# An attention and feed-forward kernel whose softmax weights are rounded and selected one head ahead of their use, with the loads and the exchange of squares moved in the step

## The chip, the cores and the metric

The kernel runs on one core of a Trainium2 chip. The metric is the device time of one execution in microseconds (us); lower is better. The core has TensorE (PE, with its weight loads as PEld), VectorE (DVE), ScalarE (ACT), GpSimd (POOL) and SyncE (SP), which here issues nearly every DMA. Each engine works through its own instructions in order and waits on semaphores for the others.

## The reference

Sliding-window attention with 4 sink keys feeds a feed-forward block, all in float32:

```python
B, H, S, D = q.shape            # 4, 8, 768, 64; n_sink 4, window 128
scores = scale * np.matmul(q, k.transpose(0, 1, 3, 2))
keep = is_sink | in_window      # the first 4 keys, or the 128 up to the query
a = softmax(np.where(keep, scores, -1e9))
x = (a @ v).transpose(0, 2, 1, 3).reshape(B * S, H * D)   # 3072 x 512
h = x @ w_in                                               # 512 x 2048
g = np.maximum(h, 0.0) + np.log1p(np.exp(-np.abs(h)))      # softplus
out = g @ w_out                                            # 2048 x 512
```

## The kernel before

The 3072 rows are cut into 12 chunks of 256 queries, three to a batch; a chunk has 8 heads. For a head, a block of 128 queries needs its own 128 keys and those of the block before, and because the window is 128 long each row keeps exactly one key of each pair (own key k, old key k); so the softmax runs on 128 + 8 columns (8 for the sinks), and the weights are later parted by a triangular select. To keep float32 accuracy, operands of matmuls are split into a rounded high part and a residue: `th` and `tl` of the transposed weights, `vv` of the values, `qkh` and `kl` of queries and keys, `gh` and `gl` of the gate, `xh` and `xl` of the attention's output.

The work is software-pipelined by hand. After an opening (`START`, a list of parts that also loads and splits the weights), a loop runs a step i for each head, and a string names the parts of a step in order; a part's number in the table `parts` says how many heads ahead of i it works. The order of the parts is the program order on every engine. Written for step i, the parts are: `L` loads query and key of head i+6, `G` the values (every second head); `p` splits the queries and keys of head i+5 (`qkh` on ACT, then `qkh`, `kl` on DVE); `S`, `T`, `N` are scores, softmax and normalisation of head i+4; `X` (swap) lets DVE transpose the normalised weights in squares of 32 into the one buffer `xf`, and SP write them to DRAM as `rows` by four DMAs; `x` (swapped) reads them back as `u`; `W` (weights_t) rounds `u` to `th` on ACT, and on POOL makes the residue `tl` and four triangular selects into `pt`, which has two buffers; `V` multiplies `pt` by the values on PE; `O` adds up and splits the output; `k` and `K` handle the sinks of four heads (`sa`, `ts`, `sk`). The dense block works 8 steps behind: `U` (up, 24 matmuls), `F` (softplus on ACT), `P` (gate), `R` (residue), and `D`, `E` (down, 6 matmuls each); the stores of a chunk's output are issued in `E`. In the opening the number stands behind the letter: `X18` is the transpose of head 18.

`xf` is one buffer, so a transpose waits until the four DMAs of the one before have read it; `u` has one buffer for even and one for odd heads; `qk` has two buffers, `vr` one.

```python
        nc.vector.transpose(squares.rearrange("p (f j q) -> p f j q", j=CH, q=32), a)
        for e in range(P // 32):
            nc.sync.dma_start(rows[:, e].rearrange("(f k) r -> k f r", k=32), src)
        # swapped:
        nc.sync.dma_start(u[:].rearrange("p e j q -> p (e j q)"), self.u[h][:].rearrange("p e r -> p (e r)"))
```

Of the kernel before, what the change touches and what calls it, by code (L numbers as in the profile page):

```python
# [20 lines left out]
B, H, S, D = 4, 8, 768, 64  # L21
# [521 lines left out]
def _weight_check(c, s, k, half):  # L543

    if not c.w64:
        return
    w = c.w[s, k, half][:, 0].rearrange("p n w -> p (n w)")  # L550
    o = 2 * (2 * s + k) + half
    for e, op in enumerate((ALU.min, ALU.max)):
        c.nc.vector.tensor_reduce(c.room[:, e, o : o + 1], w, mybir.AxisListType.X, op, apply_absolute_value=True)
# [71 lines left out]
def _fast(c):  # L625
# [6 lines left out]
    att = [_Attention(c, k) for k in range(n)]  # L632
# [3 lines left out]
    def call(lst, name, every=1, *args):  # L636
        def run(i):
            k, e = divmod(i, H)
            if 0 <= i < n * H and e % every == 0:
                getattr(lst[k], name)(e // every, *args)  # L640

        return run
# [67 lines left out]
    def idle(k):  # L710
# [11 lines left out]
        "N": (call(att, "normalise"), G),  # L722
        "p": (call(att, "split"), G + 1),
        "q": (call(att, "split_v", 2), 1),
        "W": (call(att, "weights_t"), 0),
        "X": (call(att, "swap"), 2),
        "x": (call(att, "swapped"), 1),
        "k": (call(att, "sink_weights", G), 0),
        "K": (call(att, "sink", G), 0),
        "V": (call(att, "values"), 0),  # L730
# [16 lines left out]
    with c.tc.manual_schedule():  # L747
        for h in (0, 2):
            att[0].load(h)
        _constants(c)  # L750
        att[0].load_v(0)
        att[0].load_sinks()
        att[0].load(4)
        att[0].load_v(1)
        att[0].load(6)
        c.turn = 0
        c.upper = [c.lp.tile([P, WH], I32, tag=f"vs{e}", name=f"upper{e}", bufs=1) for e in range(2)]
        for t in c.upper:
            c.nc.gpsimd.memset(t[:], 0)
        c.word_ps = [c.ps_acc.tile([P, WH], I32, tag=f"acc{e}", name=f"word_ps{e}") for e in range(2)]  # L760
        for part in c.START.split():
            parts[part[0]][0](int(part[1:] or 0))
        for i in range(2 * H + 1, (n + 1) * H + lag + 1):
            for part in "xXJjGL" + c.STEADY[i % H == 0]:
                run, ahead = parts[part]
                run(i + ahead)
            if i >= 2 * H + lag and i % 2 == 0 and checks:
                _weight_check(c, *checks.pop(0))
            if i == n * H + lag:
                for e in checks:  # L770
                    _weight_check(c, *e)
                _fast_signs(c)
            if i == n * H + 2 * lag:
                _fast_flag(c)


def _fast_signs(c):

    nc = c.nc
    c.col = col = c.const.tile([P, 3], F32, name="flag_col")  # L780
    nc.vector.tensor_reduce(col[:, 0:1], c.stats[:, : c.nchunks * CH * H], mybir.AxisListType.X, ALU.max)
    for e, (op, lim, beyond) in enumerate(((ALU.min, 2.0**-119, ALU.is_lt), (ALU.max, 2.0**121, ALU.is_ge))):
        m = col[:, e + 1 : e + 2]
        nc.vector.tensor_reduce(m, c.room[:, e], mybir.AxisListType.X, op)
        nc.vector.tensor_scalar(m, m, lim, BIG, beyond, ALU.mult)
        nc.vector.tensor_tensor(col[:, 0:1], col[:, 0:1], m, ALU.max)


def _fast_flag(c):

    nc, cp = c.nc, c.const
    row = c.ps_t.tile([1, P], F32, tag="t", name="flag_row")
    nc.tensor.transpose(row[:], c.col[:, 0:1], c.ident[:])
    f = cp.tile([1, 2], F32, name="flag_f")
    ok, u = f[:, 0:1], f[:, 1:2]
    nc.vector.tensor_reduce(ok, row[:], mybir.AxisListType.X, ALU.max)
    nc.vector.tensor_scalar(ok, ok, 9.0e8, None, ALU.is_lt)
    for src, lim, op in ((c.ns, float(NS), ALU.is_le), (c.wd, 1.0, ALU.is_ge), (c.wd, float(P), ALU.is_le)):
        nc.vector.tensor_scalar(u, src[:1], lim, None, op)
        nc.vector.tensor_tensor(ok, ok, u, ALU.mult)  # L800
    c.flag = cp.tile([1, 1], I32, name="flag_i")
    nc.vector.tensor_copy(c.flag[:], ok)
# [126 lines left out]
def _kernel(tc, a, out):  # L929
# [7 lines left out]
    with ExitStack() as keep:  # L937
# [12 lines left out]
        with ExitStack() as st:  # L950
            pool = lambda n, bufs: st.enter_context(tc.tile_pool(name=n, bufs=bufs))
            psum = lambda n, bufs: st.enter_context(tc.tile_pool(name=n, bufs=bufs, space=bass.MemoryType.PSUM))
            c.xp, c.mp, c.stg = pool("xp", 2), pool("mp", 2), pool("stg", 4)
            c.lp, c.ap, c.sp = pool("lp", 2), pool("ap", 2), pool("sp", 2)
            c.dp = st.enter_context(tc.tile_pool(name="dp", bufs=4, space=bass.MemoryType.DRAM))
            c.ps_acc, c.ps_t, c.ps_x = psum("ps_acc", 1), psum("ps_t", 1), psum("ps_x", 1)
            fronts = {}

            def scores_pool(name, bufs, to):
                side = "right" if name[-1] == "s" else "left"  # L960
                p = tc.tile_pool(name=name, bufs=bufs, space=bass.MemoryType.PSUM, side=side, reuse_waits="tile")
                return to.enter_context(p)

            def follow(name):
                fronts[name].close()
                return scores_pool(name, 2, st)

            for n in ("ps_s", "ps_h"):
                fronts[n] = st.enter_context(ExitStack())
            c.front_s, c.front_h = (scores_pool(f"front{n[2:]}", 1, own) for n, own in fronts.items())  # L970
            c.follow, c.ps_s, c.ps_h, c.idle = follow, None, None, None
            c.xf = c.sp.tile([P, 2, CT], F32, name="xf", bufs=1)
            with tc.manual_schedule(engines=ORDERED):
                _fast(c)
# [12 lines left out]
Ctx.WH = "APPPAAPAPPPPAAVAPAPAVAAVPAAAVAPA"  # L987
Ctx.WL = "PPPVVPPVPPVVVPVPVPPVVVPPVPPVVPPV"
Ctx.STEADY = (
    "kWUqYpKSFTRDVPONE",  # L990
    "SWTkpUKERDNFPqYVO",
)
Ctx.START = """
W0 N12 V14 V4 O4 V6 V0 S0 N6 V12 w j4 V2 N14 W14 O0 V10 N0 w w L8 O2 N2 S1 J0 w w w L10 L12 w T0 T1 S2 G4 w V8
# [4 lines left out]
W11 W4 T14 G16 c l c W2 D0 a d S15 d P2 l L19 U3 a L20 T15 W13 R1 E0 c l S16 c N15 D1 O9 E1 k12 R2 E2 F3 d l d  # L999
d a a T16 D2 P3 c a U4 L22 c l l a c d N16 R3 D3 d p17 c a p18 F4 d d V11 l l a K12 c d O11 a U5 N8 l l G18  # L1000
S17 F5 c T17 P4 c W10 l R4 p19 V13 O13 W15 X16 a a d S18 l a U6 E3 d T18 D4 P5 d c S19 T19 R5 l l d c p20 F6 q16 l
l P6 J16 N18 E4 V15 x16 a O15 U7 N19 S20 W16 c c c U8 D5 E5 F7 N17 X17 k16 N10 T20 R6 F8 P7 x17 X18 R7 P8 K16 E6 d d d L21 p21
a D6 N20 V16 W6 l l O16
"""


# [44 lines left out]
```

## Time and profile before

| what | value |
|---|---|
| median of 3 runs | 718.83 us (715.72 to 719.13) |
| profiled execution, its time | 718.53 us |
| its span, first to last instruction | 716.6 us |
| busy: PE, DVE, ACT, POOL | 676.0, 531.9, 476.5, 445.9 us |
| granted TensorE clock, mean | 0.993 |

The time is the span and about 2 us around it. PE is the busiest engine, and its matmuls overlap, so that a busy PE isn't one at its peak; where PE stands still, the row of the instruction that ends the wait says for how long and on whom. The opening takes the first 104 us of the span, the loop up to 660 us, and from there on only the dense block of the last chunk is left.

### The profile page before, as it was taken

Reading aid. Unit: us, or ns where it says so; the run is one execution under the profiler, and the core shown is the slowest. Engines: PE = TensorE matmul, PEld = TensorE weight load, DVE = VectorE, ACT = ScalarE, POOL = GpSimd, SP = SyncE. Lnnn points to the kernel's source line nnn. Section 1 sums busy time; section 2 is a strip of 40 time slices with the busy share of each in tenths; the row PEclk is TensorE's granted clock in tenths of the full one; section 3 lists DMA queues with packets and bytes.
Section 4 is the critical chain, followed back from the end, with each engine's and each line's share of the span. In section 5 each row is a group of like instructions: output and inputs, shape, how many; then the busy total and the mean of one; then the engine's idle time right before and its main releaser. Section 6 shows DMA issues by size and latency. Waiting matters only on the chain.

```text
span 716.6 us, 14271 instructions
## 1 busy us (share of the span) xinstructions
PE 676.0 (94%) x4319; PEld 596.2 (83%) x4319; DVE 531.9 (74%) x1461; ACT 476.5 (66%) x1213; POOL 445.9 (62%) x817
## 2 busy tenths in 40 slices
PE   6999968999999999899999989999999999999996
PEld 3588857888988889789989979888988988899995
DVE  6999947878878788778788778877788777753331
ACT  6999746767768667667777666767676676754431
POOL 7775556777666675676766676686766766674110
PEclk9999989999999999999999999999999999999999
DMA  8996124334344443433443443534433433420001
GB/s 315 362 403 177 52 61 114 99 90 126 101 105 116 116 104 91 135 94 91 130 113 93 132 111 88 146 84 111 116 97 101 134 94 96 115 67 8 30 1 34
DMA packets 97656, 83.33 MB, mean 116 GB/s; under 512 B 51876, under 2 KB 79140, under 8 KB 97572
## 3 DMA queue, kind: packets, MB, share of 16 engines
q1 hardware_dynamic: 97428, 82.35, 39.9%
q8 instruction: 36, 0.59, 0.4%
q14 instruction: 48, 0.39, 0.2%
q10 hardware_dynamic: 144, 0.00, 0.0%
HBM read 65.53 MB, written 16.78 MB: 115 GB/s over the span
## 4 chain that ended last, share of the span: by engine, by line
PE 34%; DVE 15%; ACT 14%; POOL 10%; DMA 7%; issue 6%; SPq 4%; DVEq 0%; ACTq 0%; POOLq 0%
PE h L574 16%; DMA qk<-qk 6%; PE acc L611 5%; PE acc L612 5%; PE acc L613 5%; PE x L444 3%; SPq L378 3%; ACT a L293 2%; POOL tl L67 2%; POOL pt L406 2%; POOL a L318 2%; POOL pt L409 2%; ACT mt L582 2%; DVE xt L464 2%; ACT mt L583 2%
## 5 line engine op out<-in xcount | busy, mean ns | idle before, releaser
L574 PE MATMUL h<-xh,wi 128*128 128x256 f32 x1536 | 246.7, 283 | 0.3 <-DVE mt L589 0.3
L574 PEld LDWEIGHTS h<-xh,wi 128*128 128x128 f32 x1536 | 215.7, 191 | 7.1 <-issue 0.9
L574 PE MATMUL h<-xl,wi 128*128 128x256 f32 x768 | 154.7, 283 | 0.0
L611 PE MATMUL acc<-wo,gh 128*128 128x512 f32 x384 | 153.2, 399 | 0.0
L613 PE MATMUL acc<-wo,gl 128*128 128x512 f32 x384 | 151.2, 394 | 0.7 <-DVE gl L67 0.7
L612 PE MATMUL acc<-wo,gh 128*128 128x512 f32 x384 | 151.6, 395 | 0.0
L63 POOL TENSOR_SCALAR gh<-mt 128x512 fp32r<-128x512 f32 x88 | 54.5, 619 | 140.3 <-DVE mt L589 125.1
L574 PEld LDWEIGHTS h<-xl,wi 128*128 128x128 f32 x768 | 119.6, 192 | 0.0
L581 ACT ACTIVATE mt<-h 128x512 f32<-128x512 f32 x96 | 57.4, 598 | 84.7 <-PE h L574 74.3
L318 POOL TENSOR_SCALAR a<-a,rc 128x128 f32<-128x128 f32 x156 | 60.4, 399 | 57.5 <-DVE rc L307 46.8
L589 DVE SCALAR_TENSOR_TENSOR mt<-h,mt 128x512 f32<-128x512 f32 x96 | 65.6, 684 | 41.0 <-ACT mt L583 28.1
L613 PEld LDWEIGHTS acc<-wo,gl 128*128 128x128 f32 x384 | 72.5, 189 | 18.6 <-DVE gl L67 1.9
L293 ACT ACTIVATE a<-a,stats 128x136 f32<-128x136 f32 x192 | 76.0, 397 | 16.0 <-DVE stats L292 15.6
L611 PEld LDWEIGHTS acc<-wo,gh 128*128 128x128 f32 x384 | 72.7, 189 | 12.7
L67 DVE TENSOR_TENSOR qkh<-qk,qkh 64x256 fp32r<-64x256 f32 x80 | 46.7, 584 | 46.9 <-ACT qkh L59 45.8
L612 PEld LDWEIGHTS acc<-wo,gh 128*128 128x128 f32 x384 | 72.9, 190 | 9.5
L59 ACT CAST qkh<-qk 128x656 fp32r<-128x656 f32 x80 | 59.0, 738 | 31.4 <-DMA qk<-qk 31.0
L67 DVE TENSOR_TENSOR gl<-mt,gh 128x512 fp32r<-128x512 f32 x96 | 73.6, 767 | 4.3 <-POOL gh L63 4.0
L67 POOL TENSOR_TENSOR tl<-u,th 128x256 f32<-128x256 f32 x80 | 63.7, 796 | 7.7 <-ACT th L59 7.7
L444 PE MATMUL x<-pt,vv 128*128 128x256 f32 (+1 forms) x216 | 50.4, 336 | 17.1 <-POOL pt L409 16.6
L582 ACT ACTIVATE mt<-mt 128x512 f32<-128x512 f32 x96 | 60.7, 633 | 3.1
L583 ACT ACTIVATE mt<-mt 128x512 f32<-128x512 f32 x96 | 60.7, 632 | 3.1
(193 smaller groups left out, 1203.4 us busy)
## 6 DMA issues: line engine op xcount, KB each, us to landing
qk<-qk SPq DMA_DIRECT2D x160, 164.0 KB, 3.1
rows<-xf SPq DMA_DIRECT2D x320, 32.0 KB, 1.6
u<-rows SPq DMA_DIRECT2D x80, 128.0 KB, 2.6
vr<-v SPq DMA_DIRECT2D x32, 192.0 KB, 2.7
out<-o SPq DMA_DIRECT2D x24, 256.0 KB, 2.3
qk<-qk SPq DMA_DIRECT2D x8, 328.0 KB, 6.4
vr<-v SPq DMA_DIRECT2D x16, 128.0 KB, 2.3
wi00r<-w SPq DMA_DIRECT2D x1, 511.8 KB
```

The lines of the kernel that those rows point to most:

```text
L59: nc.scalar.copy(out, in_)
L67: (nc.vector if eng == "V" else nc.gpsimd).tensor_tensor(out, a, b, ALU.subtract)
L293: nc.scalar.activation(a, a, AF.Exp, bias=nm, scale=-1.0, accum_out=total)
L318: (nc.vector if eng == "V" else nc.gpsimd).tensor_scalar(a, a, rc[:, j : j + 1], 0.0, ALU.mult, ALU.add)
L444: nc.tensor.matmul(x[:, :, o], w, pt[:, :, m], start=False, stop=n == 2, skip_group_check=True)
L574: nc.tensor.matmul(h[:, j], wt, x, start=k == 0, stop=k >= len(prods) - 2, skip_group_check=True)
L582: nc.scalar.activation(t[:], t[:], AF.Exp, scale=-1.0)
L583: nc.scalar.activation(t[:], t[:], AF.Ln, bias=1.0)
L589: nc.vector.scalar_tensor_tensor(t[:], h[:], 0.0, t[:], ALU.max, ALU.add)
L611: nc.tensor.matmul(acc[:], gh[:, j, q], wh, start=f == 0, stop=False, skip_group_check=True)
L612: nc.tensor.matmul(acc[:], gh[:, j, q], wl, start=False, stop=False, skip_group_check=True)
L613: nc.tensor.matmul(acc[:], gl[:, j, q], wh, start=False, stop=f == 2 * FP - 1, skip_group_check=True)
```

## The change

`W` works one head further ahead (i+1 where it was i), and so do `x` (i+2) and `X` (i+3). `x` and `X` no longer stand first in a step: `x` comes behind the loads `G` and `L`, and `X` stands in the middle of the step, behind `F`. The last lines of the opening are rewritten to fit: the load `L21` stands ahead of `x16`, `x17` and `X18` ahead of `T20`, and `W17`, `x18` and `X19` are now in the opening.

```diff
-        "W": (call(att, "weights_t"), 0),
-        "X": (call(att, "swap"), 2),
-        "x": (call(att, "swapped"), 1),
+        "W": (call(att, "weights_t"), 1),
+        "X": (call(att, "swap"), 3),
+        "x": (call(att, "swapped"), 2),
...
-            for part in "xXJjGL" + c.STEADY[i % H == 0]:
+            for part in "JjGLx" + c.STEADY[i % H == 0]:
...
-    "kWUqYpKSFTRDVPONE",
-    "SWTkpUKERDNFPqYVO",
+    "kWUqYpKSFTXRDVPONE",
+    "SWTkpUKERDNFXPqYVO",
...
-l P6 J16 N18 E4 V15 x16 a O15 U7 N19 S20 W16 c c c U8 D5 E5 F7 N17 X17 k16 N10 T20 R6 F8 P7 x17 X18 R7 P8 K16 E6 d d d L21 p21
-a D6 N20 V16 W6 l l O16
+l P6 J16 N18 E4 V15 L21 x16 a O15 U7 N19 S20 W16 c c c U8 D5 E5 F7 N17 X17 k16 N10 x17 X18 T20 R6 F8 P7 x18 X19 R7 P8 K16 E6 d d d p21
+a D6 N20 W17 V16 W6 l l O16
```

What this does to the engines' own orders is seen at two places. The first is a step of the loop. On POOL, in step 18 (heads of chunk 2: the number behind the tile's name is the chunk, the next one the head, or for `gh` the slice of the dense block), before:

```order
L318 TENSOR_SCALAR a2_1_1349<-a2_1_1349,rc2_1_1350 128x128 x2
L67 TENSOR_TENSOR tl2_2_1553<-u2_2_1427,th2_2_1551 128x256
L406 AFFINE_SELECT pt2_2_1555<-th2_2_1551 128x2x128
L409 AFFINE_SELECT pt2_2_1555<-th2_2_1551 128x2x128
L406 AFFINE_SELECT pt2_2_1555<-tl2_2_1553 128x2x128
L409 AFFINE_SELECT pt2_2_1555<-tl2_2_1553 128x2x128
L63 TENSOR_SCALAR gh1_2_1625<-mt1_2_1598 128x512
```

and now:

```order
L318 TENSOR_SCALAR a2_1_1360<-a2_1_1360,rc2_1_1361 128x128 x2
L67 TENSOR_TENSOR tl2_3_1564<-u2_3_1450,th2_3_1562 128x256
L406 AFFINE_SELECT pt2_3_1566<-th2_3_1562 128x2x128
L409 AFFINE_SELECT pt2_3_1566<-th2_3_1562 128x2x128
L406 AFFINE_SELECT pt2_3_1566<-tl2_3_1564 128x2x128
L409 AFFINE_SELECT pt2_3_1566<-tl2_3_1564 128x2x128
L63 TENSOR_SCALAR gh1_2_1642<-mt1_2_1609 128x512
```

The work of POOL between the normalisation and the gate is the same, but for head 3 instead of head 2. On DVE, in step 19, before:

```order
L553 TENSOR_REDUCE room_64<-wi00_343 128x1 x2
L374 STREAM_TRANSPOSE xf_105<-a2_1_1349 128x256
L67 TENSOR_TENSOR qkh3_0_1691<-qk3_0_1548,qkh3_0_1691 64x256
L67 TENSOR_TENSOR kl3_0_1694<-qk3_0_1548,qkh3_0_1691 128x400
L285 COPY_PREDICATED s2_7_0_1696<-diag_133,s2_7_0_1696 128x128
L285 COPY_PREDICATED s2_7_1_1699<-diag_133,s2_7_1_1699 128x128
L292 ISA a2_1_1349,stats_63<-s2_7_0_1696,mask2_146 128x136
...
L67 TENSOR_TENSOR gl1_2_1713<-mt1_2_1598,gh1_2_1625 128x512
```

and now:

```order
L553 TENSOR_REDUCE room_64<-wi00_343 128x1 x2
L67 TENSOR_TENSOR qkh3_0_1702<-qk3_0_1557,qkh3_0_1702 64x256
L67 TENSOR_TENSOR kl3_0_1705<-qk3_0_1557,qkh3_0_1702 128x400
L285 COPY_PREDICATED s2_7_0_1707<-diag_133,s2_7_0_1707 128x128
L285 COPY_PREDICATED s2_7_1_1710<-diag_133,s2_7_1_1710 128x128
L292 ISA a2_1_1360,stats_63<-s2_7_0_1707,mask2_146 128x136
...
L374 STREAM_TRANSPOSE xf_105<-a2_1_1360 128x256
L67 TENSOR_TENSOR gl1_2_1730<-mt1_2_1609,gh1_2_1642 128x512
```

The transpose has moved from ahead of the split to behind the softmax, and it is that of head 6 (22 in all) where it was head 5.

The second place is the end of the opening. On SP, before:

```order
L378 DMA rows2_0_1104<-xf_105 32x4x64 x4
L146 DMA vsr0_1216<-vs 128x1x128
L387 DMA u2_0_1242<-rows2_0_1104 128x256
L378 DMA rows2_1_1342<-xf_105 32x4x64 x4
L387 DMA u2_1_1367<-rows2_1_1342 128x256
L378 DMA rows2_2_1370<-xf_105 32x4x64 x4
L200 DMA qk2_5_1396<-qk 64x656 x2
L387 DMA u2_2_1427<-rows2_2_1370 128x256
```

and now:

```order
L378 DMA rows2_0_1104<-xf_105 32x4x64 x4
L146 DMA vsr0_1216<-vs 128x1x128
L200 DMA qk2_5_1242<-qk 64x656 x2
L387 DMA u2_0_1245<-rows2_0_1104 128x256
L378 DMA rows2_1_1345<-xf_105 32x4x64 x4
L387 DMA u2_1_1352<-rows2_1_1345 128x256
L378 DMA rows2_2_1355<-xf_105 32x4x64 x4
L387 DMA u2_2_1378<-rows2_2_1355 128x256
```

The load of head 21 (chunk 2, head 5) is now ahead of the first read-back `u` of the loop's heads. On DVE at the same place, before:

```order
L374 STREAM_TRANSPOSE xf_105<-a2_0_906 128x256
L323 TENSOR_TENSOR sa2_0_1347<-a2_0_906,rc2_0_907 128x64
L285 COPY_PREDICATED s2_4_0_1276<-diag_133,s2_4_0_1276 128x128
...
L67 TENSOR_TENSOR gl0_6_1358<-mt0_6_1202,gh0_6_1214 128x512
L589 SCALAR_TENSOR_TENSOR mt0_7_1333<-h0_7_1247,mt0_7_1333 128x512
L61 CAST gh0_7_1365<-mt0_7_1333 128x512
L374 STREAM_TRANSPOSE xf_105<-a2_0_906 128x256
```

and now:

```order
L374 STREAM_TRANSPOSE xf_105<-a2_0_906 128x256
L323 TENSOR_TENSOR sa2_0_1350<-a2_0_906,rc2_0_907 128x64
L374 STREAM_TRANSPOSE xf_105<-a2_0_906 128x256
L285 COPY_PREDICATED s2_4_0_1279<-diag_133,s2_4_0_1279 128x128
...
L67 TENSOR_TENSOR gl0_6_1369<-mt0_6_1202,gh0_6_1214 128x512
L589 SCALAR_TENSOR_TENSOR mt0_7_1336<-h0_7_1250,mt0_7_1336 128x512
L61 CAST gh0_7_1376<-mt0_7_1336 128x512
L374 STREAM_TRANSPOSE xf_105<-a2_0_906 128x256
```

The transposes of heads 17 and 18 now stand almost next to each other, and the softmax of head 20 and the residue `gl` behind them; that of head 19 takes the old place of head 18.

## Rows read from the trace of the kernel before

**Rows 1.** The page: busy time of each engine, and the group of value matmuls

```profile
PE 676.0 (94%) x4319; PEld 596.2 (83%) x4319; DVE 531.9 (74%) x1461; ACT 476.5 (66%) x1213; POOL 445.9 (62%) x817
...
L444 PE MATMUL x<-pt,vv 128*128 128x256 f32 (+1 forms) x216 | 50.4, 336 | 17.1 <-POOL pt L409 16.6
```

**Rows 2.** Waits of PE, 158.7 to 659.8 us: total, times, longest

```profile
PE x L444 <- POOL pt L409: 12.5, 14, 1.5
```

**Rows 3.** Waits of PE, 86 to 158.7 us

```profile
PE ts L334 <- DVE sa L323: 4.8, 1, 4.8
PE x L444 <- POOL pt L409: 4.1, 4, 1.8
```

**Rows 4.** Timeline of PE, 282 to 306 us: start, length, [idle before]

```profile
290.58 0.64 PE L574 MATMUL h<-xh,wi 128*128 128x256 f32 x4
...
297.30 0.64 PE L574 MATMUL h<-xh,wi 128*128 128x256 f32 x4
...
304.08 0.73 PE L444 MATMUL x<-pt,vv 128*128 128x256 f32 x3 [1.44 <-POOL pt L409]
...
306.04 0.52 PE L574 MATMUL h<-xh,wi 128*128 128x256 f32 x3
```

**Rows 5.** Timeline of POOL, 297 to 305.5 us

```profile
300.08 1.03 POOL L318 TENSOR_SCALAR a<-a,rc 128x128 f32<-128x128 f32 x2
...
303.17 0.86 POOL L409 TENSOR_SCALAR_AFFINE_SELECT pt<-tl 128x256 fp32r<-128x256 f32 x1
```

**Rows 6.** Timelines of DVE and ACT, 290 to 300 us

```profile
291.92 0.43 DVE L374 STREAM_TRANSPOSE xf<-a 128x256 f32<-128x256 f32 x1
294.85 0.42 DVE L67 TENSOR_TENSOR qkh<-qk,qkh 64x256 fp32r<-64x256 f32 x1 [2.51 <-ACT qkh L59]
...
296.63 0.69 DVE L67 TENSOR_TENSOR gl<-mt,gh 128x512 fp32r<-128x512 f32 x1
...
294.08 0.74 ACT L59 CAST qkh<-qk 128x656 fp32r<-128x656 f32 x1 [2.12 <-DMA qk<-qk]
```

**Rows 7.** Timeline of SP, 284 to 299 us: issues of DMAs

```profile
292.37 1.75 SPq L378 DMA_DIRECT2D rows<-xf  x4
294.22 1.13 SPq L200 DMA_DIRECT2D qk<-qk  x2
295.58 0.40 SPq L387 DMA_DIRECT2D u<-rows  x1
```

**Rows 8.** DMA issues, 269.7 to 327.4 us: count, KB each, median us to landing

```profile
qk<-qk SPq DMA_DIRECT2D x16, 164.0 KB, 3.2
rows<-xf SPq DMA_DIRECT2D x32, 32.0 KB, 1.6
u<-rows SPq DMA_DIRECT2D x8, 128.0 KB, 2.9
```

**Rows 9.** Two chunks of eight steps: length, busy PE, PEld, DVE, ACT, POOL

```profile
269.70:327.40 57.70, 54.85 (x356) 49.34 (x355) 45.51 (x124) 38.78 (x102) 40.25 (x75) 1.00 0.40 107
327.40:381.30 53.90, 53.65 (x349) 48.39 (x348) 45.26 (x124) 38.89 (x101) 36.33 (x73) 1.00 0.42 111
```

**Rows 10.** Waits of DVE, 269.7 to 327.4 us

```profile
DVE qkh L67 <- ACT qkh L59: 4.5, 5, 2.5
DVE xt L464 <- ACT xt L59: 2.8, 4, 1.0
```

**Rows 11.** Timelines of the opening's end: DVE, ACT, SP and POOL

```profile
96.28 0.45 DVE L374 STREAM_TRANSPOSE xf<-a 128x256 f32<-128x256 f32 x1 [0.76 <-ACT a L316]
...
97.05 0.48 DVE L285 COPY_PREDICATED s<-diag,s 128x128 f32<-128x128 int32 x2
...
106.62 0.74 ACT L59 CAST qkh<-qk 128x656 fp32r<-128x656 f32 x1 [4.87 <-DMA qk<-qk]
...
96.76 1.73 SPq L378 DMA_DIRECT2D rows<-xf  x4
...
99.23 1.28 POOL L67 TENSOR_TENSOR wo<-wt,wo 128x512 fp32r<-128x512 f32 x1
```

## The prediction, made before the changed kernel was run

> **What bounds the kernel now.** I read the page first: PE is busy 676.0 us of the 716.6 us span, DVE 531.9, ACT and POOL less, and of all groups of matmuls only the values `V` stand idle for long, 17.1 us, nearly all of it on POOL's last select into `pt` [rows 1]. The waits of PE by stretch say where: 12.5 us in 14 waits in the loop from 158.7 us on, where PE waits for almost nothing else [rows 2], and in the stretch of the opening's end and the first loop steps 4.1 us in 4 waits, besides 4.8 us in one wait for the sinks' `sa` [rows 3]. The timeline of PE then shows what one wait is worth: a step without it takes 297.30 - 290.58 = 6.72 us, the next one, with 1.44 us of recorded wait, 306.04 - 297.30 = 8.74 us [rows 4]. It is longer by 2.02 us, so about 0.6 us more than the record; part of that is the sinks' transpose, which stands in the second step alone, and I count 0.3 us for each wait as restart.
>
> Why `pt` is late is seen on POOL: the normalisation of the head four further on stands ahead of `W`, and the last select ends at 303.17 + 0.86 = 304.03, just when PE goes on [rows 5]. Behind that stand the loads: in the step before, ACT waits 2.12 us for `qk`, and DVE 2.51 us for ACT [rows 6]. SP issues that order in one line: four writes of squares, the next load, the read-back, 1.75 + 1.13 + 0.40 us [rows 7], and the writes wait for DVE's transpose. From the transpose at 291.92 to the landing of the load behind it go 294.22 + 1.13 + 3.2 - 291.92 = 6.6 us [rows 6 to 8], about as long as the 6.72 us step in which ACT wants it. So both waits come from places in the order that leave no margin; no engine but PE is short of time.
>
> **The change, part by part.** No instruction is added or taken away in a step of the loop, and no DMA; only places move, so busy times stay.
>
> W one step ahead. `pt` of head i+1 is made while PE needs that of head i, so `V` has a whole step, 6.7 us, of margin where the longest wait in the loop was 1.5 us [rows 2]. This takes the 14 waits: 12.5 + 14 x 0.3 = 16.7 us; with no restart 12.5, with 0.6 us each 20.9. Of the four early waits the longest, 1.8 us, belongs to the opening below; the other three give 2.3 + 0.9 = 3.2 us. The buffers allow it: the selects for head i+1 write over the `pt` that `V` read in step i-1, and POOL comes to them only after its normalisation, which ends at 301.1, 3.8 us into the step that began at 297.30 [rows 4, 5].
>
> X in the middle of the step. On SP the cycle of writes, load, read-back is the same as before; the loads come sooner only because the transpose does. In its step the new place (where `gl` starts, 296.63) is 4.7 us behind the old one (291.92), or 2.2 us without the 2.51 us wait [rows 6], and the head is one further on; so the transpose, and the load behind it, come 6.7 - 4.7 = 2.0 to 6.7 - 2.2 = 4.5 us sooner. That covers the 2.12 us wait for `qk`. `u` is wanted a step sooner, so the way from transpose to `W` has two steps less 2.2 to 4.7 us, 8.7 to 11.2 us; it needs 295.58 + 2.9 - 291.92 = 6.6 us [rows 6 to 8]. The transpose itself now needs weights normalised 3.8 us into the step, and stands 296.63 - 290.58 = 6.0 us into it: 2.2 us of margin. `xf` is free again 0.43 + 1.75 + 1.6 = 3.8 us after a transpose starts, and the next one is a step away. On DVE the transpose used to lie in the wait for ACT's `qkh`, and no longer does: 0.43 us of DVE in perhaps half the steps. That lies under PE, as long as DVE has slack: a chunk with few waits took 53.9 us with DVE busy 45.26 [rows 9].
>
> The opening. `X18` now stands right behind `X17` and `sa`, ahead of the softmax of head 20, the residue `gl` and the gate on DVE. `xf` is free when the four writes of head 17 have landed, 96.76 + 1.73 + 1.6 = 100.1 us [rows 8, 11]; so the softmax that started at 97.05 starts near 100.5, 3.5 us later, and PE's down matmuls and the first `V` wait behind it. The load `L21` (1.1 us of issue) stands ahead of `u` of head 16, whose landing starts that chain: 1.1 us at least, at most 1.1 + 3.2 us if it had to wait until the load has landed; I take 1.3, since the load is small beside what lands in such a time. Against this stands the refund: ACT's wait of 4.87 us for the load of head 21 is gone [rows 11], and with `W17` done the 1.8 us wait of `V`. Last, `W17` stands on POOL ahead of a weight's subtraction of 1.28 us [rows 11], which the down matmuls of step 17 need, and it waits for ACT to normalise head 20; I estimate 2 us. In sum: PE leaves the opening 3.5 + 1.3 - 0.8 = 4 us later (0.8 us for POOL and DVE, which stood in each other's way at that place), loses 2 us at the weight, and gets back 1.8 us at `V` and about 1.7 us of step 17's small waits and restarts: +2.5 us; bounds 0 (the refund covers it) and +6.
>
> The Trainium skill has a rule that speaks against putting a load ahead of the exchange: in "DMA: Bandwidth & Descriptors", section "Queues, rings and completion order", it says that each DMA engine takes one queue's descriptors in the order of the ring. By it `u` of head 16 would wait until the 328 KB of the load are moved, which at the 435 GB/s of the page's specifications would be 0.75 us, an estimate by that page; with the issue the term would be 1.9 us where I take 1.3, and the sum 0.6 us higher. No row before the change shows a read-back right behind such a load on an empty queue.
>
> **The sum.** From the profiled execution, 718.5 us (0.3 us below the median): 718.5 - 16.7 - 3.2 + 2.5 = 701.1; I say 701. With the ends of its terms: 718.5 - 20.9 - 3.2 - 0.9 = 693.5 to 718.5 - 12.5 - 2.3 + 6 = 709.7.
>
> **Rivals.**
> First, PE is freed but DVE with ACT sets the pace. For: their work is a ping-pong with waits of its own. In the chunk of 57.7 us DVE is idle 57.7 - 45.51 = 12.2 us; without the waits for `qkh` and `xt` [rows 9, 10] 4.9 us are left, of the 4.5 us for `qkh` perhaps 2.0 + 1.7 stay (less the longest; plus 0.43 in four steps), so 54.1 us, and with half of the 2.8 us for `xt` 55.5. Against: the chunk of 53.9 us ran with all of these. At 54.1 to 55.5 instead of some 53.9 in nine chunks the time is 703 to 715; I say 709.
>
> Second, no gain: the change does less than it says, since the cycle on SP is unchanged, and `V` waits no more but the scores do, for `qkh`. For: ACT and DVE wait for loads by hand-to-mouth margins. Against: the 2.0 us of extra margin, and the whole step at `V`. Then 716 to 721.
>
> Third, slower: the transpose in the middle of the step becomes a stop on DVE, with `gl` and the gate behind it, and PE waits at the down matmuls. The place is the `X` ahead of `R`; it decides once the normalised weights or the free `xf` come more than 2.2 or 2.9 us later than worked out above. The price is each further us in each step: DVE's 54.1 / 8 = 6.8 us a step has only 0.2 us below the mean step before ((659.8 - 158.7) / 72 = 7.0), so half a us of stop makes 0.3 x 80 = 24 us, about 740. For: the opening does just this, twice if the writes of head 18 are late too. Against: 3.8 us of work against a step of 6.7.
>
> **How the numbers follow.** PE bound as worked out: 0.73, with 693 to 710 as its own range. First rival 0.11, second 0.07, third 0.09. The range 692 to 711 holds most of the first case and half of the first rival. Half a per cent, 3.6 us, is about what a measurement here tells from no change: faster takes the first case and most of the first rival, 0.83; same 0.08; slower 0.09.
>
> **What would show it.** Right: `V` waits near 0 in the loop, ACT's waits for `qk` and `vr` small, chunks of 52.5 to 54.5 us each, the opening some us longer with DVE waiting at `X18` for the writes of head 17. Wrong: DVE waits at `X` in every step, ACT waits at `th` for `u`, or PE waits at the scores, the down matmuls or the sinks instead.

## The result, and the profile after

The changed kernel takes 695.91 us (median of 4 runs, 695.47 to 696.68), the kernel before 718.41 us: a ratio of 0.9695, 95% interval 0.9668 to 0.9721. The prediction was 701 us, 692 to 711. The profiled execution took 695.82 us with a span of 694.1 us.

The page of the changed kernel: busy time of each engine, and the chain that ended last by engine.

```profile
PE 667.8 (96%) x4319; PEld 597.1 (86%) x4319; DVE 525.6 (76%) x1461; ACT 470.8 (68%) x1213; POOL 451.4 (65%) x817
...
PE 83%; POOL 0%; DVE 0%; issue 0%
```

The chain that ended last, which the view follows back to 111.49 us, is now PE almost alone; before, PE had 34% of the span in it, DVE 15%, ACT 14%. PE does the same 4319 matmuls in 8.2 us less busy time than in [rows 1], a point that comes back below. Waits of PE are left only at the opening's end; from 158.7 to 637 us the view of waits lists none. All its waits from 86 to 158.7 us (total, times, longest):

```profile
PE ts L334 <- DVE sa L323: 6.1, 1, 6.1
PE acc L613 <- DVE gl L67: 3.6, 1, 3.6
PE acc L612 <- POOL wo L67: 0.5, 1, 0.5
```

Against [rows 3] the four waits of `V` are gone, the wait for the sinks' `sa` is 1.3 us longer, and the down matmuls wait 3.6 us for the residue `gl` and 0.5 us for a weight.

The waits of ACT and DVE from 158.7 to 637 us for DMAs:

```profile
ACT th L59 <- DMA u<-rows: 9.5, 7, 2.2
```

ACT waits for no load of `qk` or `vr` any more, and in 7 steps of 72 for `u`. The same two chunks as in [rows 9], with the same columns:

```profile
264.32:318.14 53.82, 53.82 (x357) 49.35 (x355) 44.48 (x124) 38.27 (x102) 40.61 (x75) 1.00 0.43 115
318.14:371.07 52.93, 52.93 (x349) 48.47 (x348) 44.46 (x124) 38.06 (x101) 37.52 (x73) 1.00 0.42 113
```

They take 53.82 and 52.93 us where they took 57.70 and 53.90, and PE is busy for all of it.

Where the 22.7 us of the two profiled executions come from is read from the first `up` matmul of a step (L574). Step 18 begins its dense block at 114.77 us before and at 116.74 us after: the opening lost 2.0 us. Steps 18 to 23 take 158.67 - 114.77 = 43.90 us before and 157.50 - 116.74 = 40.76 us after, 3.1 us less. The 72 steps from 24 to 95 lie between these rows of the timeline of PE, before:

```profile
114.77 0.40 PE L574 MATMUL h<-xh,wi 128*128 128x256 f32 x2
...
158.67 0.40 PE L574 MATMUL h<-xh,wi 128*128 128x256 f32 x2
...
659.76 0.52 PE L574 MATMUL h<-xh,wi 128*128 128x256 f32 x3
```

and after:

```profile
116.74 0.28 PE L574 MATMUL h<-xh,wi 128*128 128x256 f32 x1
...
157.50 0.28 PE L574 MATMUL h<-xh,wi 128*128 128x256 f32 x1
...
637.28 0.40 PE L574 MATMUL h<-xh,wi 128*128 128x256 f32 x2
```

That is 501.09 us before and 479.78 us after: 21.3 us less, 6.960 against 6.664 us a step. The tail behind is as long as before (56.9 and 56.8 us). In sum 2.0 - 3.1 - 21.3 = -22.4 us.

### The profile page after: what moved, and what is told of

Its sections match the earlier page's. It is cut to its first block, busy times and chain, and to the rows that moved or that the text cites. A ratio compares the mean times of both kernels' runs of the same rounds, so it can differ in the third digit from the quotient of the medians.

```text
span 694.1 us, 14210 instructions
## 1 busy us (share of the span) xinstructions
PE 667.8 (96%) x4319; PEld 597.1 (86%) x4319; DVE 525.6 (76%) x1461; ACT 470.8 (68%) x1213; POOL 451.4 (65%) x817
## 4 chain that ended last, share of the span: by engine, by line
PE 83%; POOL 0%; DVE 0%; issue 0%
PE h L574 36%; PE acc L612 12%; PE acc L611 12%; PE acc L613 12%; PE x L444 5%; PE s L263 3%; PE s L264 3%; PE x L438 1%; PE ts L334 0%; POOL wo L67 0%; DVE o L61 0%; POOL pt L409 0%; POOL pt L406 0%; PE flag_row L793 0%
## 5 line engine op out<-in xcount | busy, mean ns | idle before, releaser
L574 PE MATMUL h<-xh,wi 128*128 128x256 f32 x1536 | 246.9, 283 | 0.3 <-DVE mt L589 0.3
L574 PEld LDWEIGHTS h<-xh,wi 128*128 128x128 f32 x1536 | 215.9, 191 | 7.1 <-issue 0.9
L574 PE MATMUL h<-xl,wi 128*128 128x256 f32 x768 | 154.7, 283 | 0.0
L574 PEld LDWEIGHTS h<-xl,wi 128*128 128x128 f32 x768 | 119.7, 192 | 0.0
L318 POOL TENSOR_SCALAR a<-a,rc 128x128 f32<-128x128 f32 x156 | 61.9, 409 | 33.0 <-DVE rc L307 32.7
L612 PEld LDWEIGHTS acc<-wo,gh 128*128 128x128 f32 x384 | 72.9, 190 | 10.2 <-POOL wo L67 0.9
L67 DVE TENSOR_TENSOR gl<-mt,gh 128x512 fp32r<-128x512 f32 x96 | 76.9, 801 | 4.4 <-POOL gh L63 4.0
L67 POOL TENSOR_TENSOR tl<-u,th 128x256 f32<-128x256 f32 x80 | 65.8, 823 | 14.6 <-ACT th L59 14.5
L67 DVE TENSOR_TENSOR qkh<-qk,qkh 64x256 fp32r<-64x256 f32 x80 | 42.8, 535 | 40.5 <-ACT qkh L59 39.3
L67 DVE TENSOR_TENSOR kl<-qk,qkh 128x400 fp32r<-128x400 f32 x80 | 52.0, 649 | 2.1
```

What stands on the lines that cost most here:

```text
L67: (nc.vector if eng == "V" else nc.gpsimd).tensor_tensor(out, a, b, ALU.subtract)
L318: (nc.vector if eng == "V" else nc.gpsimd).tensor_scalar(a, a, rc[:, j : j + 1], 0.0, ALU.mult, ALU.add)
L574: nc.tensor.matmul(h[:, j], wt, x, start=k == 0, stop=k >= len(prods) - 2, skip_group_check=True)
L612: nc.tensor.matmul(acc[:], gh[:, j, q], wl, start=False, stop=False, skip_group_check=True)
```

## The experiments

Each diff is against the changed kernel, except where it says otherwise. "The 72 steps" are those just counted, read in the same way. Each ratio is to runs of the kernel before that were taken beside that kernel (medians 717.29 to 718.41 us).

| run | what it is | time, us | ratio to before, 95% | the 72 steps, us |
|---|---|---|---|---|
| before | | 718.41 | | 501.1 |
| the change | | 695.91 | 0.9695 [0.9668, 0.9721] | 479.8 |
| e1_w_only | `W` ahead, `X` in its old place | 727.86 | 1.0158 [1.0120, 1.0196] | 512.8 |
| e2_x_only | loads first and `X` moved, `W` not ahead | 707.21 | 0.9857 [0.9829, 0.9884] | 490.4 |
| e5_loads_first | before, loads first alone | 709.90 | 0.9887 [0.9865, 0.9909] | 493.6 |
| e6_x_after_o | the change, `X` behind `O` | 709.30 | 0.9905 [0.9869, 0.9941] | 492.8 |
| e3_x18_back | the change, `X18` in its old place, `X19` later | 696.21 (one run) | | 480.5 |
| e4_l21_behind | the change, `L21` behind `x16` | 694.03 (one run) | | 479.9 |
| e7_g18_behind | the change, `G18` behind `x16` | 691.20 (one run) | | 480.3 |
| e8_opening_all | all of the opening's moves | 686.64 | 0.9569 [0.9554, 0.9584] | 479.9 |
| e9_x_first3 | e8 with `X` first in the step | 700.30 | 0.9766 [0.9746, 0.9786] | 491.9 |
| e10_x_behind_p | e8 with `X` behind `P` | 687.85 | 0.9592 [0.9571, 0.9612] | 480.5 |

### W ahead alone

The transposes stand first in the step again and two heads ahead; `W` stays one head ahead, and the read-back `x` behind the loads. The opening's end is fitted to it.

```diff
-        "X": (call(att, "swap"), 3),
+        "X": (call(att, "swap"), 2),
...
-            for part in "JjGLx" + c.STEADY[i % H == 0]:
+            for part in "XJjGLx" + c.STEADY[i % H == 0]:
...
-    "kWUqYpKSFTXRDVPONE",
-    "SWTkpUKERDNFXPqYVO",
+    "kWUqYpKSFTRDVPONE",
+    "SWTkpUKERDNFPqYVO",
```

> The weights are rounded and selected a step ahead as in the change, but the transposes keep their old place at the start of a step (head i+2), and the opening is fitted to that. Theory (the gain is the margin of a whole step at the value matmuls): PE waits at V for less than 1 us in all in the loop, ACT still waits 10 us or more for query and key loads, and may now wait for u, since a transpose has one step less on its way to W; the loop from step 24 on takes 480 to 484 us as after the change, the time is 694 to 699 us. Rival (the late loads were the cause, W ahead only moves the wait to the scores or down matmuls): PE waits over 8 us in the loop at other places, time 704 to 716 us.

Measured: 727.86 us, 1.0158 [1.0120, 1.0196], slower than the kernel before, which neither theory had expected. `V` waits no more, but from 158.7 to 640 us these do:

```profile
PE ts L334 <- DVE sa L323: 18.9, 15, 2.2
...
ACT th L59 <- DMA u<-rows: 78.4, 39, 4.3
```

The timelines of DVE, SP and ACT in this run, from 302 to 325 us, put together in the order of the chain:

```profile
302.69 0.45 DVE L374 STREAM_TRANSPOSE xf<-a 128x256 f32<-128x256 f32 x1
...
303.17 2.00 SPq L378 DMA_DIRECT2D rows<-xf  x4
305.21 0.67 SPq L220 DMA_DIRECT2D vr<-v  x1
305.98 1.11 SPq L200 DMA_DIRECT2D qk<-qk  x2
307.26 0.45 SPq L387 DMA_DIRECT2D u<-rows  x1
...
310.17 0.41 ACT L59 CAST th<-u 128x256 fp32r<-128x256 f32 x1 [2.23 <-DMA u<-rows]
310.89 0.74 ACT L59 CAST qkh<-qk 128x656 fp32r<-128x656 f32 x1
...
311.66 0.43 DVE L67 TENSOR_TENSOR qkh<-qk,qkh 64x256 fp32r<-64x256 f32 x1 [1.36 <-ACT qkh L59]
...
316.80 0.45 DVE L374 STREAM_TRANSPOSE xf<-a 128x256 f32<-128x256 f32 x1
...
324.16 0.41 ACT L59 CAST th<-u 128x256 fp32r<-128x256 f32 x1 [2.24 <-DMA u<-rows]
```

It is a loop with no slack. From the transpose to the start of ACT's `th` go 310.17 - 302.69 = 7.48 us: the writes, two loads in SP's queue, the read-back. ACT's `qkh` stands behind the `th` that had to wait; DVE waits for `qkh`, does a step's work behind it, and comes to the transpose of the head two further on at 316.80, 6.63 us later. Two steps take 324.16 - 310.17 = 13.99 us where PE alone needs 2 x 6.66. With `W` a step earlier and `X` where it was, the exchange has one step, and it needs more than one. Part of the 11.7 us by which the 72 steps are longer than before may be TensorE's clock: in these 72 steps it is granted at its lower level, 1.2 GHz, for 10.2 us in all, where before and after the change it stays at 2.4 GHz.

### X and the loads alone

Here `X` stands where the change puts it and the loads stand first on SP; `W` works on its own step's head, with `x`, still two heads ahead, behind it.

```diff
-        "W": (call(att, "weights_t"), 1),
+        "W": (call(att, "weights_t"), 0),
...
-            for part in "JjGLx" + c.STEADY[i % H == 0]:
+            for part in "JjGL" + c.STEADY[i % H == 0]:
...
-    "kWUqYpKSFTXRDVPONE",
-    "SWTkpUKERDNFXPqYVO",
+    "kWxUqYpKSFTXRDVPONE",
+    "SWxTkpUKERDNFXPqYVO",
```

> The transposes, writes and loads come early as in the change (head i+3 in the middle of the step), but W works on the head of its own step, as before; the read-back stands behind W. Theory (margin at V): ACT's waits for loads are near 0, yet the selects still end where PE comes to V, so V waits go on, 6 to 12 us on record in the loop, and the time is 704 to 714 us. Rival (early loads are the cause): V waits under 2 us, time 694 to 699 us.

Measured: 707.21 us, 0.9857 [0.9829, 0.9884]. The time is where the theory had it; the waits of `V` are shorter than its 6 to 12 us. The one wait of PE that is left from 158.7 to 640 us:

```profile
PE x L444 <- POOL pt L409: 4.4, 8, 0.7
```

So 8 of the 14 waits of `V` in [rows 2] stay, and are shorter; half of the loop's gain, 10.7 of 21.3 us, has come without moving `W` ahead.

### The loads first, and nothing else

The kernel before, with one line changed: what a step puts on SP begins with the loads, then the read-back, then the writes.

```diff
-            for part in "xXJjGL" + c.STEADY[i % H == 0]:
+            for part in "JjGLxX" + c.STEADY[i % H == 0]:
```

> The kernel before with one edit: in a step of the loop the loads stand ahead of the read-back and the squares on SP, so that the load of head i+6 no longer follows the transpose of head i+2; DVE, ACT, POOL and PE keep the old order. Theory after e1 and e2 (two loops of about 14 us per two steps hold the kernel before, one through transpose, load, ACT and DVE, one through V, up, softplus, normalisation, selects and V again; each must go): ACT's waits for qk go to under 6 us, the V waits stay in part, mean step of the loop 6.78 to 6.88 us as in e2 (6.81) and time 705 to 711 us. Rival A (loads do not matter): 716 to 720 us. Rival B (loads are all): 694 to 698 us.

Measured: 709.90 us, 0.9887 [0.9865, 0.9909], as expected: 7.5 us of the 72 steps for an order of issue on one queue. In the kernel before, ACT's waits for loads from 157 to 640 us were these:

```profile
ACT qkh L59 <- DMA qk<-qk: 23.2, 30, 2.1
ACT vv L59 <- DMA vr<-v: 13.7, 10, 2.5
```

With the loads first none of them is left, and the waits of `V` from 158.7 to 640 us have halved against [rows 2]:

```profile
PE x L444 <- POOL pt L409: 6.7, 12, 1.4
```

### The transpose later in the step

```diff
-    "kWUqYpKSFTXRDVPONE",
-    "SWTkpUKERDNFXPqYVO",
+    "kWUqYpKSFTRDVPOXNE",
+    "SWTkpUKERDNFPqYVOX",
```

> The changed kernel with the transpose later in the step, behind the output's additions (X behind O instead of behind F), still head i+3 and W a step ahead. In e1 the way transpose, writes, load, read-back, ACT, DVE, transpose took 14.1 us for two steps, 7.05 us a step. Here it is shorter by the reciprocal with its wait, the tensor reductions and part of the rest, about 13.0 to 13.4 us, 6.5 to 6.7 us a step beside PE's 6.66. Theory (the loop decides, with a threshold at PE's step): 695 to 701 us. Rival (the later the transpose, the slower, without a threshold: more than half of the way from behind the softmax to e1's place): 708 to 722 us.

Measured: 709.30 us, 0.9905 [0.9869, 0.9941]. The theory's estimate missed; the time fell where the rival had put it. The waits from 158.7 to 640 us of PE and, for `u`, of ACT:

```profile
PE ts L334 <- DVE sa L323: 8.4, 9, 1.9
...
ACT th L59 <- DMA u<-rows: 66.6, 35, 3.4
```

The waits are those of e1_w_only again: 35 for `u` where the change has 7. That the time rises with each later place, without a limit, was the other half of the rival; e10_x_behind_p below bears on it.

### The transpose earlier, or a little later

Both runs start from e8_opening_all (below), whose loop is as long as that of the change. In the first, `X` of head i+3 stands first in the step's work of DVE, and behind the loads and the read-back on SP; in the second it stands behind `P`.

```diff
-            for part in "JjGLx" + c.STEADY[i % H == 0]:
+            for part in "JjGLxX" + c.STEADY[i % H == 0]:
...
-    "kWUqYpKSFTXRDVPONE",
-    "SWTkpUKERDNFXPqYVO",
+    "kWUqYpKSFTRDVPONE",
+    "SWTkpUKERDNFPqYVO",
```

> The version with the whole opening moved (686.64 us; mean step in the loop 6.665 us), with X first in the step's work of DVE instead of behind F, still three heads ahead. The transpose then comes about 2.0 us sooner in the step (the normalised weights end on POOL at 290.82 in that trace, the transpose stood at 292.46). Theory (the exchange is a chain that must be back within two steps, and PE sets the pace once it is): no wait for u is left, DVE waits at the transpose for POOL by 0.3 to 0.8 us in many steps, and that lies under PE: mean step 6.64 to 6.69, 685 to 689 us. Rival (the prediction's third: the transpose is a stop on DVE, with the split of queries and keys behind it): each half us of stop adds 0.1 to 0.3 us to the step, 6.77 to 6.95, 694 to 707 us.

Measured: 700.30 us, 0.9766 [0.9746, 0.9786]; the rival was right. The waits of PE and DVE from 158.7 to 640 us that are new:

```profile
PE ts L334 <- DVE sa L323: 7.6, 14, 1.6
...
DVE xf L374 <- POOL a L318: 34.2, 37, 1.2
DVE xf L374 <- DMA rows<-xf: 6.2, 6, 2.4
```

and one of them in the timelines of POOL and DVE:

```profile
288.75 0.72 POOL L318 TENSOR_SCALAR a<-a,rc 128x128 f32<-128x128 f32 x2
...
289.50 0.45 DVE L374 STREAM_TRANSPOSE xf<-a 128x256 f32<-128x256 f32 x1 [1.15 <-POOL a L318]
```

The weights of head i+3 are normalised by POOL at the very end of the step before. A transpose that stands first in the step waits for them, and holds the split of queries and keys behind it. The 34.2 + 6.2 = 40.4 us of waits at the transpose cost 491.9 - 479.9 = 12.0 us in 72 steps, 0.3 us for each us of stop; how much of it passes through the 7.6 us for `sa` wasn't tried apart.

```diff
-    "kWUqYpKSFTXRDVPONE",
-    "SWTkpUKERDNFXPqYVO",
+    "kWUqYpKSFTRDVPXONE",
+    "SWTkpUKERDNFPXqYVO",
```

> The same version with X behind P, between the place of the change (behind F) and the one behind O, where the loop's mean step was 6.844 us. Theory (the exchange as a chain back to the same place two steps later): the transpose is 0.7 us later in the step for the residue gl and some more for the gate, so ACT waits for u in part of the steps, more than 8 and fewer than 35; mean step 6.68 to 6.78, 688 to 696 us. Rival (the place behind O was slow for what stands around it on DVE and PE, not for the exchange): 6.66 to 6.67 as now, 686 to 688 us, with no more waits for u than before.

Measured: 687.85 us, 0.9592 [0.9571, 0.9612], with 10 waits for `u`; 480.5 us for the 72 steps, 6.673 us a step. The time is the rival's, under the theory's range by some 0.01 us a step; the waits for `u` are 10 where e8_opening_all has 8, just in the theory's. Behind `P` the exchange still fits, and a later place alone doesn't slow the loop much; behind `O` the 35 waits for `u` say that it fits no longer, though what else stands around that place on DVE and PE, this run's rival, wasn't tried apart. So the place has a limit on both sides, the weights of POOL ahead and, as far as shown, the way of the exchange behind, and from behind F to behind P it costs only 0.6 us in the 72 steps.

### The end of the opening

One part of the opening's end is put back or moved in each of three runs, and all of them together, with `W17` behind the weights, in a fourth.

```diff
-... N17 X17 k16 N10 x17 X18 T20 R6 F8 P7 x18 X19 R7 P8 K16 E6 ...
+... N17 X17 k16 N10 T20 R6 F8 P7 x17 X18 R7 P8 K16 x18 X19 E6 ...
```

> The changed kernel with the transposes of heads 18 and 19 in the opening put back behind the softmax and gate (X18) and behind the sinks (X19). Theory (the two transposes next to each other stop DVE for the four writes): DVE's wait of 2.97 us at X18 and PE's 3.56 us at the down matmuls go, PE starts step 18 at 113.5 to 115 us where it was 116.74, time 1.5 to 3 us lower than the changed kernel's 695.9. Rival (another chain, the weight behind W17 or the load of head 21, ends as late): step 18 starts at 116 us or later, no gain.

Measured: 696.21 us in one run, no change, as the rival had it: step 18 starts at 116.05 us. Of DVE's waits for the writes 0.8 us is left and of that of PE for `gl` 0.2 us, but PE then waits for the weight that stands behind `W17` on POOL:

```profile
PE acc L612 <- POOL wo L67: 2.4, 1, 2.4
```

The next run exchanges the load and the read-back:

```diff
-... V15 L21 x16 a O15 ...
+... V15 x16 L21 a O15 ...
```

> The changed kernel with the load of head 21 in the opening put behind the read-back of head 16 on SP. The read-back is then issued 0.7 us sooner (91.20 to 90.5 us). If only the issue counted, ACT starts on u of head 16 at 93.8 us where it was 94.55. If the read-back also waits behind the load's bytes on the DMA engines, it starts at 92.9 us as before the change, 1.6 us sooner, and step 18 starts 1.6 us sooner, at 115.1 us; time about 694.3.

Measured: 694.03 us in one run, as expected for the case that the load's bytes count too. In the change SP issues the load ahead of `u`, and ACT starts `th` of head 16 at 94.55 us, the start of the late chain:

```profile
86.80 0.38 SPq L220 DMA_DIRECT2D vr<-v  x1
87.23 1.91 SPq L378 DMA_DIRECT2D rows<-xf  x4
...
89.89 1.14 SPq L200 DMA_DIRECT2D qk<-qk  x2
91.20 0.45 SPq L387 DMA_DIRECT2D u<-rows  x1
...
94.55 0.40 ACT L59 CAST th<-u 128x256 fp32r<-128x256 f32 x1 [7.07 <-DMA u<-rows]
```

With the load behind, in this run:

```profile
90.52 0.35 SPq L387 DMA_DIRECT2D u<-rows  x1
...
92.61 0.40 ACT L59 CAST th<-u 128x256 fp32r<-128x256 f32 x1 [5.10 <-DMA u<-rows]
```

`u` is issued 0.68 us sooner, and used 1.94 us sooner: 3.35 us after its issue behind the load, 2.09 us without it. So 1.3 us of the cost comes after the issue; only the load's place was changed, so I put it down to the load's transfer.

The rows of the change show more: the writes of head 16's squares, issued at 87.23 us, stand behind a load of values at 86.80 us, `G18`. The view of waits of SP's own queue, from 70 to 105 us, shows that it stands still for 8.9 us until POOL has read the one buffer of the load before (9.0 us in the kernel before, so this is not the change's doing):

```profile
SPq L220 <- POOL vv L67: 8.9, 1, 8.9
```

The third run puts `G18` behind `x16`:

```diff
-... a U5 N8 l l G18
+... a U5 N8 l l
...
-l P6 J16 N18 E4 V15 L21 x16 a O15 ...
+l P6 J16 N18 E4 V15 L21 x16 G18 a O15 ...
```

> The changed kernel with one load of values in the opening (G18) put behind the read-back of head 16 on SP. In the changed kernel this load waits until 86.8 us for its buffer, and the writes of head 16, transposed at 77 us, wait behind it until 87.23. Theory: they go out near 78 us, u of head 16 is there before ACT wants it at 87.5 us, ACT's 7.07 us wait and PE's 6.13 us wait at ts shrink to under 2 us, step 18 starts at 110 to 113 us instead of 116.74, time 689 to 692.5. Rival (the chain from there on ends as late by another way, the four writes between X17 and X18 or the weight behind W17): step 18 starts at 115 us or later.

Measured: 691.20 us in one run, as expected, with step 18 at 111.65 us. The fourth run takes all of it:

```diff
-... a U5 N8 l l G18
+... a U5 N8 l l
...
-l P6 J16 N18 E4 V15 L21 x16 a O15 ... N10 x17 X18 T20 R6 F8 P7 x18 X19 R7 P8 K16 E6 ...
-a D6 N20 W17 V16 W6 l l O16
+l P6 J16 N18 E4 V15 x16 L21 G18 a O15 ... N10 T20 R6 F8 P7 x17 X18 R7 P8 K16 x18 X19 E6 ...
+a D6 N20 V16 W6 l l W17 O16
```

> The changed kernel with all four edits of the opening: G18 and L21 behind the read-back of head 16, X18 and X19 back behind the gate and the sinks, W17 behind the weight's subtraction. If each wait is its own, step 18 starts at 108 to 111 us where it was 116.74, and the time is 687 to 691 us, faster than the change. If they share one chain, e7's gain is all there is.

Measured: 686.64 us, 0.9569 [0.9554, 0.9584], better than both kernels. The writes of head 16 are issued at 78.03 us instead of 87.23, and ACT finds `u` there:

```profile
78.03 1.96 SPq L378 DMA_DIRECT2D rows<-xf  x4
...
87.59 0.40 ACT L59 CAST th<-u 128x256 fp32r<-128x256 f32 x1
```

The loop is as long as that of the change (479.9 against 479.8 us), so the 9.3 us come from ahead of it: step 18 starts at 105.06 us, sooner than the 108 to 111 expected, and steps 18 to 23 give 2.3 us of that back. The three parts tried alone sum to 6.3 us; `W17` behind the weights wasn't tried alone, and the granted clock differs too (below).

## Why the prediction was right, and where its terms were off

**The waits of V.** They went, as worked out, and PE sets the pace: no engine took its place. The term was too small: 16.7 us, with 20.9 as its bound, where the 72 steps gave 21.3. The record holds 12.5 us in 14 waits [rows 2]; the remaining 8.8 us are 0.63 us a wait, where I took 0.3 us and had 0.6 us as the upper end. The record leaves out some of what PE loses: in the 72 steps PE stands idle for 13.5 us before and not at all after, and is busy for 487.6 and 479.8 us with the same work, so 7.8 of the 21.3 us lay in busy time. In the kernel before, the timeline of PE shows two steps, the columns as in [rows 4]:

```profile
226.07 0.64 PE L574 MATMUL h<-xh,wi 128*128 128x256 f32 x4
...
230.82 0.28 PE L438 MATMUL x<-sk,vs 128*128 128x256 f32 x1
231.11 0.74 PE L444 MATMUL x<-pt,vv 128*128 128x256 f32 x3
233.08 0.63 PE L574 MATMUL h<-xh,wi 128*128 128x256 f32 x4
...
237.83 0.28 PE L438 MATMUL x<-sk,vs 128*128 128x256 f32 x1
237.94 0.63 PE L444 MATMUL x<-pt,vv 128*128 128x256 f32 x3
239.79 0.40 PE L574 MATMUL h<-xh,wi 128*128 128x256 f32 x2
```

The first step takes 7.01 us, the second 6.71 us. In the first `V` starts 0.29 us after the sinks' matmul (L438), in the second 0.11 us, and its three matmuls take 0.74 against 0.63 us: 0.29 us of lateness without a wait in the row, since the matmul ahead is drawn 0.28 us long in both steps and fills the gap. This is where most of the 8.2 us of busy time, 7.8 us, went.

**What takes the waits away.** The whole term was put down to `W`, and the earlier loads were given no gain. The runs part it otherwise: the loads first on SP give 7.5 us, with `X` in mid-step 10.7 us, and `W` ahead the other 10.6 us. Alone, `W` ahead costs 11.7 us. That a step of margin at `V` is enough by itself is the reason that fell in e1_w_only: the margin is taken from `u`. So the loop's term came near for a reason that was only half of the cause; it did so because the change moves the loads and `X` too.

**X in the middle of the step.** The two limits named in the prediction exist, and both were met when `X` was moved off its place. The need of the exchange, 6.6 us in the prediction, was 7.5 us in the rows of e1_w_only. In the change 8.4 to 10.6 us go from the transpose to `th` in the 72 steps, 9.45 us in the median, and in 64 of them ACT doesn't wait at `th`. The seven waits for `u`, and an eighth that the view puts down to POOL, are all of head 4 of a chunk, where, and nowhere else, the stores of a chunk's output stand on SP ahead of the read-back; the prediction's sum of the need had left them out. For head 36, transposed at 221.43 us, the rows of SP and ACT are:

```profile
225.09 0.83 SPq L622 DMA_DIRECT2D out<-o  x2
...
231.82 0.41 ACT L59 CAST th<-u 128x256 fp32r<-128x256 f32 x1 [2.00 <-DMA u<-rows]
```

The margin of the weights on POOL's side held. The loads came sooner and ACT's 36.9 us of waits for them went, as expected.

**The opening.** +2.5 us predicted, +2.0 us measured. This row of the changed kernel's DVE answers to its largest term, `X18`:

```profile
101.45 0.45 DVE L374 STREAM_TRANSPOSE xf<-a 128x256 f32<-128x256 f32 x1 [2.97 <-DMA rows<-xf]
```

`X18` waits 2.97 us for the writes of head 17 (3.5 predicted). The weight behind `W17` cost PE 0.5 us and not 2, but only because PE was late itself: without the stop at `X18`, in e3_x18_back, it was 2.4 us. The load ahead of `u` cost 1.9 us where 1.3 was taken. That is the sum that the prediction gave for the rule in the Trainium skill ("DMA: Bandwidth & Descriptors", "Queues, rings and completion order"), by which each DMA engine takes a queue's descriptors in the order of the ring; the traces agree, with 1.3 us between issue and use more than without the load. The parts of that sum were otherwise, 0.7 us of issue where 1.1 was taken and 1.3 us behind it where the estimate was 0.75, so its fit is partly luck. The three early waits of `V` were worth 3.1 us where 3.2 was predicted.

One thing is counted in neither the prediction nor the experiments: TensorE's granted clock. The same view as in [rows 9], from 95 to 110 us before and after, has its mean third from the end:

```profile
95.00:110.00 15.00, 11.02 (x50) 8.57 (x51) 9.27 (x23) 7.17 (x21) 7.21 (x12) 0.77 0.23 57
95.00:110.00 15.00, 7.90 (x24) 5.75 (x25) 7.90 (x23) 8.26 (x22) 3.41 (x9) 0.54 0.18 44
```

The clock is at its lower level, 1.2 GHz, from 95.40 to 102.23 us before and from 95.72 to 109.38 us after; on either side it is at 2.4 GHz. It falls while PE stands still for `sa`, from 92.38 to 97.18 us before and from 92.41 to 98.54 us after, and in the changed kernel PE stands still again, for `gl`, up to 103.37 us. The down matmuls start 0.43 us apart at the lower level and 0.23 us apart at the upper. From these and the other distances between starts I estimate that the lower level cost at most 2.1 us before and 3.5 us after. So part of the 2.0 us may be the clock, and that the opening's sum came out near is in part luck. In e7_g18_behind the stretch at the lower level is 6.8 us long, and in e8_opening_all, where PE no longer waits for `sa` there, the clock stays at 2.4 GHz; what of their gains is the clock wasn't tried apart.

**The rivals.** DVE and ACT as the pace: chunks of 53.8 and 52.9 us, so no. No gain: no. The transpose as a stop on DVE: not where the change puts it; in e9_x_first3 it was there, at 0.3 us for each us of stop, about half the price that the prediction worked out.

**What stays open.** Whether the 9.5 us that ACT still waits for `u` in 7 steps cost PE anything wasn't tried; no wait of PE goes with them. How the opening's time divides between its waits and the clock stays open too.

## What to carry to other kernels

Where the product of one step is wanted by a queue that feeds the next, follow the whole way round, in program order, until it returns to the same place two steps later, and compare it with as many steps of the bottleneck: here, moving the last link of the chain forward alone lost 11.7 us, and with its first link moved too it gained. On SP here a transfer that waited for its buffer held those issued behind it; look first at what stands ahead of the one that is late. And where PE waits briefly and often, count the lengths of steps with and without the wait, not the idle time of the record.

## What the runs showed of the hardware that was not expected

In one step 0.29 us of PE's lateness don't appear as idle time, and of the 21.3 us that went from the 72 steps the record of before had 12.5 us as waits of `V`. A read-back of 128 KB was used 2.09 us after its issue, and 3.35 us after it when a load of 328 KB in two DMAs had been issued just ahead (one run without the load). One DMA on SP that waited 8.9 us for its buffer held writes whose squares DVE had transposed at 77.11 us until 87.23 us, and to move it was worth about 4.7 us of the kernel's time (695.91 to 691.20 in one run), more than either of the opening's other parts tried alone, with 6.8 us of TensorE at the lower clock where the change has 13.7 us.
